# An attention, Fourier mixing and feed-forward kernel on one core: thirteen plain attention tiles instead of eighteen, a fused mask, and weights put together on VectorE

## The chip, the core and the metric

The kernel runs on one core of a Trainium2 chip. A core has a matrix engine (TensorE, PE in the profile), a vector engine (VectorE, DVE), an activation engine (ScalarE, ACT), a general engine (GpSimd, POOL) and a queue engine that issues transfers (SyncE, SP). Each works through its own list of instructions in a fixed order and waits on semaphores for the others. PEld is the loading of the stationary operand into PE. The metric is the device time of one launch in microseconds; the time of the kernel before is the median of three runs.

## What is computed

```python
# q, k, v: (8, 8, 576, 64); w_ch1: (512, 2048); w_ch2: (2048, 512)
scores = (q @ k^T) / 8, kept where 0 <= i - j < 64, else -1e9
attn = softmax(scores)                      # over the last axis
x = (attn @ v), heads side by side          # (8, 576, 512)
u = x + real(fft(fft(x, axis=1), axis=2))
un = (u - mean(u)) / sqrt(var(u) + 1e-6)    # over the last axis
out = u + relu(un @ w_ch1) @ w_ch2
```

The weights arrive as 64-bit numbers (two 32-bit words, low and high); the kernel makes 32-bit floats of them itself.

## The kernel before

**Tiles.** The 8 x 576 rows are 36 tiles of 128 rows, nine to a pair of batches (tile T has place n = T mod 9 in its pair). `attn_tile` does one of them in two halves of 64 queries. It loads k, q and v, brings k and q into the layout that PE wants, multiplies (psc), takes a row's largest score and exponentials (pr), turns the probabilities round (pt), multiplies by v (pa) and normalises (xu). It then takes a radix-4 step for the Fourier part (y) and turns y round (py, yT).

**Plain tiles and tiles in parts.** Tiles below `PRO` (18 here) are plain: float32 all through, with k, q, the probabilities and y turned by TensorE (pk, pq, pp, py). The mask of a plain tile is one more product into the scores' bank (line 542): an identity times the mask, four heads wide. The row maximum is a reduction and a small scaling on VectorE (lines 573 and 574, `top`). Tiles from `PRO` on split each number into two float16 parts, high and low. Their turning is done by transposing DMAs on SP's queue (kst, qbd, pt, py), the splitting by ScalarE, VectorE and GpSimd; their mask is added on VectorE, in the fused step that also takes the row's extreme value (line 564, `masked`). Of these tiles only those whose n stands in `Y_SOON` have y turned by TensorE.

**Fourier part and normalisation.** When a pair's tiles 0 to 4, and then 5 to 8, are done, `fft` transforms one batch (products pg, pz), writes the result to memory (md), and `norm_tile` gathers the rows of it again (mt), adds them to xu, normalises, splits into parts (un, up) and turns them by a DMA into uhl, the input of the feed-forward part.

**Feed-forward part.** `ffn(c)` handles a chunk of 256 rows: 16 steps of a first product (ph, line 1186), relu into parts (hh, lines 1201 and 1204) and a second product (po, line 1167). Chunk 0 is plain (`PLAIN = 1`) and uses the weights in float32; chunks 1 to 17 use weights scaled and split into float16 parts. Chunk c takes tiles 2c and 2c + 1.

**Weights.** Each of the 32 pieces (`weight_piece`) is loaded, its high words shifted and masked by two VectorE instructions (lines 1078 and 1083), its low words scaled by ScalarE (line 1088) and added by GpSimd as 32-bit integers (line 1091). ScalarE then squares the piece for the scale; when all 16 pieces of a matrix are in, `weight_scale` makes the scale and `weight_split` the parts.

**What sets the order.** All of this is handed to a planner (`Plan`), a list of operations with a duration, a priority (a smaller number is sooner), what they read and write, and the rings of buffers they take from. It plays the operations through and writes each engine's instructions in the order that comes out; some operations may go to either of two engines, and `LAZY` and its kin say how much sooner the second must be. `slack` adds to the time at which the planner lets TensorE use what others make. The feed-forward products have the last priority, so they fill TensorE wherever a tile is not ready. Before the first of them stands in the order, warming products (warm, line 1265) are put where the planner sees TensorE idle.

## Time and profile before

| | |
|---|---|
| median of three runs | 1029.38 us (1027.97 to 1029.58) |
| profiled execution, whole | 1027.26 us |
| its span, first to last instruction | 1025.4 us |
| mean granted TensorE clock | 0.994 of full speed |
| first product of feed-forward chunk 0 | at 95.4 us |
| first product of chunk 1 (parts) | at 175.7 us |

The profile is of one execution. Busy time counts an instruction from its start to its modelled end, and TensorE's instructions overlap; so what a group of products costs is read from the distance between its first start and the start of what follows, not from their durations.

### The profile page before, as it was taken

The numbers are of one execution on the slowest core, as the hardware profiler recorded it, in microseconds if no ns is written. First come the engines' busy times: TensorE is split into PE (matmuls) and PEld (weight loads), VectorE is DVE, ScalarE is ACT, GpSimd is POOL, SyncE is SP. The second block draws the span as 40 slices with busy tenths as digits, with TensorE's granted clock in tenths as the row PEclk, the third lists the DMA queues.
The fourth block names the chain that finished last, engine by engine and source line by source line (L and its number), as shares of the span: only waits on it lengthen the run. The fifth ranks groups of instructions, "written<-read, shape, count | busy, mean of one in ns | idle before, by whom it ended". The sixth has DMA issues, their size and how long they took to land.

```text
span 1025.4 us, 22178 instructions
## 1 busy us (share of the span) xinstructions
PE 989.6 (97%) x8743; PEld 709.4 (69%) x8743; DVE 676.6 (66%) x1743; ACT 416.9 (41%) x1060; POOL 188.5 (18%) x200
## 2 busy tenths in 40 slices
PE   8788999999999999989999999999999999999998
PEld 7677767677776767666676676666676667666664
DVE  5799898798756495765775757778686754532121
ACT  5777766545424263233453225343453222211111
POOL 2124432121023020311123203032112100210000
PEclk9999999999999999999999999999999999999999
DMA  8979953337238156486798456686763511220000
GB/s 196 227 187 246 228 164 108 81 74 144 58 96 159 43 100 146 90 166 106 141 134 169 108 104 114 118 174 136 127 114 88 117 20 55 62 53 21 1 22 21
DMA packets 279032, 115.83 MB, mean 113 GB/s; under 512 B 260744, under 2 KB 260872, under 8 KB 278928
## 3 DMA queue, kind: packets, MB, share of 16 engines
q1 hardware_dynamic: 276208, 105.50, 49.9%
q0 software_dynamic: 2720, 8.92, 3.2%
q8 instruction: 69, 1.13, 0.5%
q14 instruction: 35, 0.29, 0.1%
HBM read 54.97 MB, written 14.17 MB: 67 GB/s over the span
## 4 chain that ended last, share of the span: by engine, by line
PE 71%; DVE 12%; DMA 10%; ACT 2%; SPq 2%; issue 2%; POOL 1%; DVEq 0%; ACTq 0%; POOLq 0%
PE ph L1186 31%; PE po L1167 28%; PE pa L646 2%; PE pz L899 2%; PE pg L867 2%; DMA uhl<-up 2%; DMA flex<-in_moe_w_ch 2%; DMA wd<-in_moe_w_ch 2%; PE psc L552 1%; DMA pt<-flex 1%; DVE y L680 1%; DMA va<-in_v 1%; DVE hh L1204 1%; DMA mt<-md,gix 1%; PE psc L545 1%
## 5 line engine op out<-in xcount | busy, mean ns | idle before, releaser
L1186 PE MATMUL ph<-uhl,w0s 128*128 128x256 f16 (+1 forms) x3384 | 426.6, 277 | 9.4 <-DVE hh L1204 9.2
L1167 PE MATMUL po<-w1s,hh 128*128 128x512 f16 (+1 forms) x1696 | 426.8, 389 | 0.0
L1186 PEld LDWEIGHTS <-w0s 128*128 128x128 f16 x3264 | 318.1, 98 | 94.9 <-issue 13.1
L1204 DVE SCALAR_TENSOR_TENSOR hh<-ph,hh 128x256 f16<-128x256 f32 x272 | 114.8, 423 | 235.3 <-ACT hh L1201 223.0
L1201 ACT ACTIVATE hh<-ph 128x256 f16<-128x256 f32 x272 | 104.0, 382 | 401.4 <-PE ph L1186 290.1
L1167 PEld LDWEIGHTS <-hh 128*128 128x128 f16 x1632 | 157.0, 98 | 138.3 <-issue 1.1
L977 POOL DMA_INDIRECT mt<-md,gix x34 | 34.3, 1008 | 111.3 <-DMA md<-mp 90.4
L1001 POOL TENSOR_TENSOR rs<-mv,mhalf 128x1 f32<-128x1 f32 x36 | 21.8, 606 | 178.2 <-DVE mv L997 161.5
L580 ACT ACTIVATE pr<-pr,nm 128x128 f32<-128x128 f32 x144 | 45.6, 390 | 5.7 <-DVE nm L564 5.7
L580 ACT ACTIVATE pr<-psc,nm 128x128 f32<-128x128 f32 x144 | 40.4, 380 | 16.6 <-DVE nm L574 12.5
L545 PEld LDWEIGHTS psc<-kst,qbd 128*128 128x128 f32 x288 | 37.5, 192 | 5.6 <-issue 1.7
L646 PE MATMUL pa<-ve,pt 128*64 128x65 f16 (+1 forms) x720 | 40.9, 209 | 0.1
L646 PE MATMUL pa<-va,pt 128*64 128x65 f16 (+1 forms) x720 | 40.5, 209 | 0.3 <-ACT pt L403 0.2
L545 PE MATMUL psc<-kst,qbd 128*128 128x128 f32 x288 | 38.4, 277 | 1.7 <-ACT qbd L403 1.2
L609 POOL TENSOR_TENSOR flex<-pr,flex 128x512 f16<-128x512 f32 x19 | 23.0, 1215 | 91.5 <-DVE flex L407 54.2
L482 POOL TENSOR_TENSOR flex<-kn,flex 128x512 f16<-128x512 f32 x15 | 17.6, 1176 | 117.8 <-ACT flex L403 92.3
L564 DVE CUSTOM_DVE_ANT_0 pr<-psc,mskb 128x128 f32<-128x128 f32 x144 | 32.8, 285 | 1.4 <-PE psc L552 1.4
L658 DVE TENSOR_TENSOR xu<-pa,rc 128x256 f32<-128x256 f32 x72 | 30.6, 425 | 2.5
L899 PE MATMUL pz<-g,ds__76 97*96 97x257 f16 (+3 forms) x240 | 29.1, 273 | 1.6 <-ACT pr L580 1.1
L680 DVE TENSOR_TENSOR y<-xu 128x256 f32<-128x256 f32 x66 | 29.7, 491 | 1.4 <-PE py L739 0.9
L899 PEld LDWEIGHTS <-ds__76 97*96 97x96 f16 (+1 forms) x240 | 26.8, 124 | 4.2 <-issue 2.6
L403 ACT CAST up<-un 128x512 f16<-128x512 f32 x28 | 17.2, 616 | 28.2 <-DMA uhl<-up 14.3
(155 smaller groups left out, 1214.9 us busy)
## 6 DMA issues: line engine op xcount, KB each, us to landing
wd<-in_moe_w_ch SPq DMA_DIRECT2D x20, 512.0 KB, 4.1
...
```

Source lines behind the costliest of these rows:

```text
L545: nc.tensor.matmul(p_[:, hp], qw, keys(hp, jj), start=False, stop=(hp == 3))
L564: nc.vector.tensor_tensor_reduce(out=t["pr", jj][:, hp], in0=t["ps", jj][:, hp], in1=mskb[:, m : m + P], scale=-0.125, scalar=3.0e38, op0= ...
L580: nc.scalar.activation(pr, src, AF.Exp, bias=t["nm", jj][:, hp : hp + 1], scale=sc_)
L646: nc.tensor.matmul(pa[64 * jj : 64 * jj + 64, hh], pt[:, sl], v_, start=(x == 0), stop=(x == len(mm) - 1))
L658: nc.vector.tensor_tensor(out=xv[:, 4 * hf : 4 * hf + 4], in0=pa[:, :, 0:64], in1=rc.to_broadcast([P, 4, 64]), op=ALU.mult)
L680: eng.tensor_tensor(out=o, in0=p0, in1=p1, op=al)
L899: nc.tensor.matmul(pz[:M, c0:c1], ds_[:NJ, a, c[0] : c[0] + c[1]], t["g", gi][:, b_, c0:c1], start=(x == 0), stop=(x == len(mm) - 1),)
L977: nc.gpsimd.indirect_dma_start(out=mts[T], out_offset=None, in_=mds[pb][0 : HR if n < 4 else 2 * HR], in_offset=bass.IndirectOffsetOnAxis( ...
L1167: nc.tensor.matmul(t["po"][i], l_, r_, start=(f == 0 and x == 0), stop=(f == NKF - 1 and x == len(mm) - 1))
L1186: nc.tensor.matmul(ph, l_, r_, start=(x == 0), stop=(x == len(mm) - 1))
L1201: nc.scalar.activation(t["hh", f][:, 0], ph, AF.Relu)
L1204: nc.vector.scalar_tensor_tensor(out=hh[:, 1], in0=ph, scalar=0.0, in1=hh[:, 0], op0=ALU.max, op1=ALU.subtract)
```

## The change

The change does five things. `PRO` becomes 13: tiles 13 to 17 are done in parts. Since the first tile in parts (13) now is not the first of a pair, two bridges are added: `k_tail` splits the previous tile's keys on VectorE, and `v_next` splits its values there. The mask product of the plain tiles is gone; all tiles use the fused VectorE step. The low words of a weight piece are scaled and added by one VectorE instruction that writes the lower 16 bits of each number; the ScalarE and GpSimd steps are gone. y of tiles with n = 3 is turned by DMA in tiles done in parts. And the numbers that the planner goes by are new.

```diff
-Y_SOON = (3,4,8,)
-LAZY, LAZY_FFT, LAZY_U = 0.2, 0.8, 0.2
-LAZY_E, LAZY_Y = 0.3, 0.4
+Y_SOON = (4, 8)
+LAZY, LAZY_FFT, LAZY_U = 0.4, 0.4, 0.5
+LAZY_E, LAZY_Y = 0.3, 0.8
...
-EARLY, LATER = 80, 0
-PRO = 18
-SLACK = 1.0
+EARLY, LATER = 80, -20
+PRO = 13
+PITCH, FFT_AT, NORM_AT, FFT1 = 8.5, 13, 6, 0
+SLACK = 0.5
...
-W_DMA, W_DMA_STEP, W_CONV, W_SQ, W_SPLIT, W_STEP = -40, 1.25, 40, 80, 60, 0.5
+W_DMA, W_DMA_STEP, W_CONV, W_SQ, W_SPLIT, W_STEP = -40, 1.0, 20, 60, 60, 0.3
...
+        before = (T + 1 if T == PRO else T - 1) % 3
...
+        if T == PRO and n > 0:
+            def k_tail():
+                src = kst32[:, (T - 1) % 3 * 512 : (T - 1) % 3 * 512 + 512].rearrange("p (a s) -> p a s", a=4)
+                dst = kst16[:, before * 1024 : before * 1024 + 1024].rearrange("p (h s) -> p h s", h=H)
+                for h in range(2):
+                    old = src[64 * h : 64 * h + 64, :, 64:128]
+                    hi, lo = (dst[64 * z : 64 * z + 64, h::2, 64:128] for z in range(2))
...
+                    nc.vector.tensor_copy(hi, old)
+                    nc.vector.tensor_tensor(out=lo, in0=old, in1=hi, op=ALU.subtract)
+            op("DVE", 1.6, base + 0.3, k_tail, [BkT[(T - 1) % 3]], [BkT[before], Buf("tail")])
...
         def v_next():
-            nc.sync.dma_start(vbuf[3 - i][64:128], vbuf[i][64:128])
+            if T + 1 == PRO:
+                (hi, lo), v_ = (ve[1 - i][64:128, z] for z in range(2)), va32[i][64:128]
+                nc.vector.tensor_scalar(out=hi, in0=v_, scalar1=VS, scalar2=None, op0=ALU.mult)
+                nc.vector.scalar_tensor_tensor(out=lo, in0=v_, scalar=VS, in1=hi, op0=ALU.mult, op1=ALU.subtract)
+            else:
+                nc.sync.dma_start(vbuf[3 - i][64:128], vbuf[i][64:128])
...
             def score(jj=jj, m=m):
...
-                if whole:
-                    nc.tensor.matmul(p_, idb, mskb[:, None, m : m + P].to_broadcast([P, 4, P]), start=True, stop=False)
                 for hp in range(4 if whole else 0):
                     qw = qbd32[i][:, hp, jj].rearrange("p h s -> p (h s)")
-                    nc.tensor.matmul(p_[:, hp], qw, keys(hp, jj), start=False, stop=(hp == 3))
+                    nc.tensor.matmul(p_[:, hp], qw, keys(hp, jj), start=True, stop=True)
...
-            def top(jj=jj):
-                mx, nm = (sm.tile([P, 4], F32, tag=tag, name=f"{tag}{T}_{jj}") for tag in ("mx", "nm"))
-                t["nm", jj] = nm
-                nc.vector.tensor_reduce(out=mx, in_=t["ps", jj], axis=AX.X, op=ALU.max)
-                nc.vector.tensor_scalar(out=nm, in0=mx, scalar1=-0.125, scalar2=None, op0=ALU.mult)
...
-            if whole:
-                op("DVE", 0.85, base + 2.1 + jj, top, [bs], [bnm], port=False)
-                op("ACT", 1.07, base + 2.5 + jj, expo, [bs, bnm], [bp])
-            else:
-                op("DVE", 0.86, base + 2.1 + jj, masked, [bs, Bmskb], [bp, bnm], port=False)
-                op("ACT", 1.2, base + 2.5 + jj, expo, [bnm], [bp])
+            op("DVE", 0.84, base + 2.1 + jj, masked, [bs, Bmskb], [bp, bnm], port=False)
+            op("ACT", 1.18, base + 2.5 + jj, expo, [bnm], [bp])
...
-            elif i == 2:
-                nc.scalar.mul(lo, lo.bitcast(U32), 2.0**-29)
             else:
-                nc.gpsimd.tensor_tensor(out=dst, in0=dst, in1=lo, op=ALU.add)
+                half_ = wf[x][g].bitcast(U16)[:, 0::2]
+                nc.vector.scalar_tensor_tensor(
+                    out=half_, in0=lo.bitcast(U32), scalar=2.0**-29, in1=half_, op0=ALU.mult, op1=ALU.add
+                )
...
-        op("ACT", 0.58, pr, lambda: conv(2), bw, [br])
-        op("POOL", 1.3, pr - 0.2, lambda: conv(3), [*bw, br], [bf])
+        op("DVE", 0.6, pr - 0.2, lambda: conv(2), bw, [bf])
...
-        base = 8.5 * T + (LATER if T > 4 else -EARLY)
-        plan.slack = SLACK if T >= PRO else 0.0
+        base = PITCH * T + (LATER if T > 4 else -EARLY)
+        plan.slack = SLACK if T >= NT else 0.0
```

How the order changes is shown at three places. First TensorE, at the scores of tile 0 (psc0_0 and psc0_1 are the two halves, mskb the mask, kst the keys). Before:

```order
L542 MATMUL psc0_0_155<-mskb_71,idb_72 128x512
L545 MATMUL psc0_0_155<-kst_80,qbd0_77 128x128 x4
L542 LDWEIGHTS idb_72
L542 MATMUL psc0_1_167<-mskb_71,idb_72 128x512
L545 MATMUL psc0_1_167<-kst_80,qbd0_77 128x128 x4
L462 MATMUL pk1_188<-ident_69,kn1_146 128x128 x4
L595 MATMUL pp0_0_199<-ident_69,pr0_0_154 128x128 x4
```

and after:

```order
L568 MATMUL psc0_0_153<-kst_79,qbd0_76 128x128 x4
L568 MATMUL psc0_1_160<-kst_79,qbd0_76 128x128 x4
L464 MATMUL pk1_172<-ident_69,kn1_134 128x128 x4
L464 MATMUL pq1_186<-ident_69,qn1_144 128x128 x4
L606 MATMUL pp0_0_198<-ident_69,pr0_0_152 128x128 x4
```

The product from the mask and the load of its identity are gone; the four products of the scores stand alone.

Second VectorE, at the weight pieces during the first transform (w0s and w1s hold the weights as they are put together, wd and flex are loaded pieces, mx5_1 and mx6_0 row maxima, pr5_1 the second half of tile 5, pz0 and mp0 belong to the transform). Before:

```order
L1078 TENSOR_SCALAR w1s_86<-flex_79 128x512
L1083 SCALAR_TENSOR_TENSOR w1s_86<-flex_79,w1s_86 128x512
L1078 TENSOR_SCALAR w1s_86<-wd1_3_771 128x512
L573 TENSOR_REDUCE mx6_0_970<-psc6_0_939 128x4
L574 TENSOR_SCALAR nm6_0_971<-mx6_0_970 128x4
L407 COPY qbd1_78<-pq7_931 64x8x64
L1083 SCALAR_TENSOR_TENSOR w1s_86<-wd1_3_771,w1s_86 128x512
L1078 TENSOR_SCALAR w0s_85<-wd0_4_818 128x512
```

and after:

```order
L1101 SCALAR_TENSOR_TENSOR w1s_85<-wd1_3_775,w1s_85 128x512
L1089 TENSOR_SCALAR w0s_84<-wd0_4_886 128x512
L1094 SCALAR_TENSOR_TENSOR w0s_84<-wd0_4_886,w0s_84 128x512
L1101 SCALAR_TENSOR_TENSOR w0s_84<-wd0_4_886,w0s_84 128x512
L1089 TENSOR_SCALAR w0s_84<-wd0_5_949 128x512
L1094 SCALAR_TENSOR_TENSOR w0s_84<-wd0_5_949,w0s_84 128x512
L1101 SCALAR_TENSOR_TENSOR w0s_84<-wd0_5_949,w0s_84 128x512
L1089 TENSOR_SCALAR w0s_84<-wd0_6_1036 128x512
L1094 SCALAR_TENSOR_TENSOR w0s_84<-wd0_6_1036,w0s_84 128x512
L1101 SCALAR_TENSOR_TENSOR w0s_84<-wd0_6_1036,w0s_84 128x512
L587 ISA pr5_1_707,nm5_1_1071<-psc5_1_708,mskb_71 128x128
L587 ISA nm5_1_1071 128x1
```

Each piece now has a third VectorE instruction (line 1101), and four pieces in a row stand ahead of the masked scores of tile 5's second half.

Third SP, from the last piece of transform 3 (mp3_0, written to md1) to the turn of tile 13's normalised rows (up13 into uhl6, the input of feed-forward chunk 6). Before:

```order
L927 DMA md1_3561<-mp3_0_5087 96x512
L929 DMA md1_3561<-mp3_0_5087 1x512
L497 DMA_TRANSPOSE qbd0_77<-flex_79 128x16x64
L427 DMA qn24_5220<-in_q 128x8x64
L1229 DMA out_0<-xu8_1461 128x512
L1229 DMA out_0<-xu9_1637 128x512
L524 DMA ve0_83<-va1_82 64x520
L754 DMA_TRANSPOSE py18_5386<-yp18_5369 128x8x128
L615 DMA_TRANSPOSE pt19_0_5402<-flex_79 128x8x64 x2
L615 DMA_TRANSPOSE pt19_1_5456<-flex_79 128x8x64
L1029 DMA_TRANSPOSE uhl6_4123<-up13_5430 128x8x128
```

and after:

```order
L940 DMA md1_3910<-mp3_0_5677 1x512
L427 DMA qn24_5818<-in_q 128x8x64
L499 DMA_TRANSPOSE qbd1_77<-flex_78 128x16x64
L427 DMA flex_78<-in_v 64x8x64 x2
L765 DMA_TRANSPOSE py19_5868<-yp19_5835 128x8x128
L626 DMA_TRANSPOSE pt20_0_5889<-flex_78 128x8x64
L540 DMA ve1_83<-va1_81 64x520
L499 DMA_TRANSPOSE qbd1_77<-flex_78 128x16x64
L626 DMA_TRANSPOSE pt20_0_5889<-flex_78 128x8x64
L427 DMA kn25_5931<-in_k 128x8x64
L626 DMA_TRANSPOSE pt20_1_5979<-flex_78 128x8x64
L1040 DMA_TRANSPOSE uhl6_4764<-up13_5963 128x8x128
```

The number of transfers between the two is much the same. On TensorE it is another thing: before, transform 3 stands in chunk 4 of the feed-forward part (its last product between steps of f = 12), now it stands in chunk 5 (its last product between steps 8 and 9). Between its last product and the first product of chunk 6 now stand 7 groups of ph (12 products each), 9 of po (6 products each), one tile's output products and two halves of scores.

In all, the changed program has 129 warming products (103 before; 50 of them stand in a row, between transform 0's last product and the turning of tile 5's second half), 36 mask products fewer, and 20 py, 20 pk, 20 pq and 40 pp flips fewer on TensorE. On VectorE 32 instructions of line 1101 are new and ten float32 copies of whole tiles or halves (qbd, kst, pt) are gone.

## Rows read from the trace of the kernel before

**Rows 1.** The page, part 1: busy us (share of the span) x instructions.

```profile
PE 989.6 (97%) x8743; PEld 709.4 (69%) x8743; DVE 676.6 (66%) x1743; ACT 416.9 (41%) x1060; POOL 188.5 (18%) x200
```

**Rows 2.** Windows: stretch, then its length and each engine's busy time, clock, DMA share, GB/s.

```profile
25.00:95.40 70.40, 56.40 (x611) 48.78 (x605) 62.64 (x153) 52.95 (x142) 19.17 (x17) 0.95 0.89 217
95.40:175.70 80.30, 77.35 (x502) 58.22 (x499) 70.98 (x140) 53.84 (x134) 29.13 (x23) 1.00 0.71 176
175.70:1025.40 849.70, 834.01 (x7452) 584.75 (x7450) 529.80 (x1423) 296.85 (x751) 135.07 (x146) 1.00 0.48 96
```

**Rows 3.** Waits of PE, whole program: us in total, times, longest.

```profile
PE ph L1186 <- DVE hh L1204: 9.2, 9, 2.7
```

**Rows 4.** Timeline of PE, 16 to 19 us: start, us, engine, line, operation.

```profile
16.74 0.38 PE L542 MATMUL psc<-mskb,idb 128*128 128x512 bf16 x1
16.96 1.05 PE L545 MATMUL psc<-kst,qbd 128*128 128x128 f32 x8
...
17.85 0.60 PE L462 MATMUL pk<-ident,kn 128*128 128x128 f32 x4
18.31 0.63 PE L739 MATMUL py<-ident,y 128*128 128x128 f32 x4
```

**Rows 5.** Timeline of PE, first and last of tile 3's output products.

```profile
39.41 0.27 PE L646 MATMUL pa<-ve,pt 128*64 128x65 f32 x1
...
40.34 0.22 PE L646 MATMUL pa<-ve,pt 128*64 128x65 f32 x1
```

**Rows 6.** Timeline of PE, tiles 20 to 23, done in parts.

```profile
471.50 0.22 PE L646 MATMUL pa<-ve,pt 128*64 128x65 f16 x1
...
472.28 0.62 PE L552 MATMUL psc<-kst,qbd 128*64 128x128 f16 x16
...
487.25 0.64 PE L552 MATMUL psc<-kst,qbd 128*64 128x128 f16 x16
487.82 1.47 PE L1167 MATMUL po<-w1s,hh 128*128 128x512 f16 x6
```

**Rows 7.** DVE by form, 20 to 265 us: count | busy us, mean ns | idle before.

```profile
L573 DVE TENSOR_REDUCE mx<-psc 128x4 f32<-128x512 f32 x27 | 18.5, 684 | 1.6 <-PE psc L545 1.6
...
L680 DVE TENSOR_TENSOR y<-xu 128x256 f32<-128x256 f32 x24 | 13.1, 587 | 1.0 <-PE py L739 0.9
...
L1083 DVE SCALAR_TENSOR_TENSOR w0s<-wd,w0s 128x512 int32<-128x512 int32 x9 | 6.2, 685 | 0.1
...
L407 DVE COPY qbd<-pq 64x512 f32<-64x512 f32 x7 | 4.8, 689 | 1.5 <-PE pq L462 1.3
```

**Rows 8.** Timeline of DVE, one masked half tile, first row and the next operation.

```profile
492.97 0.28 DVE L564 CUSTOM_DVE_ANT_0 pr<-psc,mskb 128x128 f32<-128x128 f32 x1
...
493.81 0.75 DVE L680 TENSOR_TENSOR y<-xu 128x256 f32<-128x256 f32 x2
```

**Rows 9.** Timelines of DVE and POOL near 83 us.

```profile
82.70 1.84 DVE L680 TENSOR_TENSOR y<-xu 128x256 f32<-128x256 f32 x2
...
82.92 1.35 POOL L1091 TENSOR_TENSOR w0s<-w0s,flex 128x512 int32<-128x512 int32 x1 [2.50 <-DMA mt<-mp]
```

**Rows 10.** Timelines, from a transform's last product to the turn of u; DMA table's row.

```profile
393.52 0.83 PE L899 MATMUL pz<-g,ds__76 97*97 97x257 f16 x6
...
396.79 1.48 PE L1186 MATMUL ph<-uhl,w0s 128*128 128x256 f16 x12
...
399.39 1.47 PE L1186 MATMUL ph<-uhl,w0s 128*128 128x256 f16 x12
...
425.61 1.26 SPq L1029 DMA_TRANSPOSE uhl<-up  x1
...
861.65 0.83 PE L899 MATMUL pz<-g,ds__76 97*97 97x257 f16 x6
...
878.77 22.13 SPq L1029 DMA_TRANSPOSE uhl<-up  x4
...
uhl<-up SPq DMA_TRANSPOSE x34, 3.3
```

More of the change, by code (lines that the diff above doesn't have):

```diff
@@ L17 @@
 U32 = mybir.dt.uint32
+U16 = mybir.dt.uint16
 AF = mybir.ActivationFunctionType
@@ L323, in attn_fft_ffn_kernel @@
     mskb = cp.tile([P, 320], BF16, name="mskb")
-    idb = cp.tile([P, P], BF16, name="idb")
     unit = cp.tile([P, P], F32, name="unit")
@@ L353, in attn_fft_ffn_kernel @@
     wp = [w_[:, 0:16].bitcast(F16).rearrange("p g (z c) -> p g z c", z=2) for w_ in ws]
-    Bid, Bmh, Bmskb, Bgix, Bdd, Bds, Bones, Bidb = (Buf() for _ in range(8))
+    Bid, Bmh, Bmskb, Bgix, Bdd, Bds, Bones = (Buf() for _ in range(7))
     Bq, Bva, Bve = ([Buf() for _ in range(2)] for _ in range(3))
@@ L380, in to_parts @@
         for i in range(2):
-            fresh = i == PRO % 2
+            fresh = PRO % NT == 0 and i == PRO % 2
             def ones(i=i, fresh=fresh):
@@ L387, in ones @@
                     nc.gpsimd.memset(ve[i][64:128], 0.0)
-            op("POOL", 0.7, 100, ones, writes=[Bva[i], Bve[i]] if fresh else [Bva[i]])
+            op("POOL", 0.7, PITCH * PRO - 25, ones, writes=[Bva[i], Bve[i]] if fresh else [Bva[i]])
     def pieces(src, b0, g0, n):
@@ L450, in keys @@
             w = kw // 64
-            own, old = T % 3 * w + 2 * h, (T - 1) % 3 * w + 2 * h + 1
+            own, old = T % 3 * w + 2 * h, before * w + 2 * h + 1
             step = old - own
@@ L505, in attn_tile @@
                 op("DMA", TURN, base + 0.7, lambda j=j: q_turn(j), Bfl[4:6], [Bq[i]], lat=2.8)
+        if T == PRO and n > 0:
[5 more added lines that the diff above has]
+                    hi, lo = (dst[64 * z : 64 * z + 64, h::2, 64:128] for z in range(2))
+                    if h:
+                        odd = sb([P, 4, 64], F32, "tail", f"odd{T}")[0:64]
+                        nc.vector.tensor_copy(odd, old)
+                        old = odd
+                    nc.vector.tensor_copy(hi, old)
+                    nc.vector.tensor_tensor(out=lo, in0=old, in1=hi, op=ALU.subtract)
+            op("DVE", 1.6, base + 0.3, k_tail, [BkT[(T - 1) % 3]], [BkT[before], Buf("tail")])
         def v_part(z):
@@ L523, in v_next @@
         def v_next():
-            nc.sync.dma_start(vbuf[3 - i][64:128], vbuf[i][64:128])
+            if T + 1 == PRO:
[4 more added lines that the diff above has]
+                nc.sync.dma_start(vbuf[3 - i][64:128], vbuf[i][64:128])
         op("DMA", 0.55, base - 4 if whole else base + 3.2, v_own, [Bva[i]], [Bve[i]], lat=2.8)
-        if n + 1 < NT:
+        if n + 1 < NT and T + 1 == PRO:
+            op("DVE", 1.1, base + 6, v_next, [Bva[i]], [Bve[1 - i]])
+        elif n + 1 < NT:
             op("DMA", 0.55, base - 3.9 if whole else base + 6, v_next, [Bva[i]], [Bve[1 - i]], lat=2.8)
@@ L555, in score @@
                             )
-            rd = [Bq[i], bkT, *([] if jj or n == 0 else [BkT[(T - 1) % 3]])]
-            op("PE", 1.15 if whole else 0.6, base + 2 + jj, score, [*rd, Bidb, Bmskb] if whole else rd, [bs, bp])
+            rd = [Bq[i], bkT, *([] if jj or n == 0 else [BkT[before]])]
+            op("PE", 0.95 if whole else 0.52, base + 2 + jj, score, rd, [bs, bp])
             def masked(jj=jj, m=m):
@@ L578, in expo @@
                     pr = t["pr", jj][:, hp]
-                    src, sc_ = (t["ps", jj][:, hp], 0.125) if whole else (pr, -1.0)
-                    nc.scalar.activation(pr, src, AF.Exp, bias=t["nm", jj][:, hp : hp + 1], scale=sc_)
-            if whole:
-                op("DVE", 0.85, base + 2.1 + jj, top, [bs], [bnm], port=False)
-                op("ACT", 1.07, base + 2.5 + jj, expo, [bs, bnm], [bp])
-            else:
-                op("DVE", 0.86, base + 2.1 + jj, masked, [bs, Bmskb], [bp, bnm], port=False)
-                op("ACT", 1.2, base + 2.5 + jj, expo, [bnm], [bp])
+                    nc.scalar.activation(pr, pr, AF.Exp, bias=t["nm", jj][:, hp : hp + 1], scale=-1.0)
+            op("DVE", 0.84, base + 2.1 + jj, masked, [bs, Bmskb], [bp, bnm], port=False)
+            op("ACT", 1.18, base + 2.5 + jj, expo, [bnm], [bp])
             if whole:
@@ L1074, in conv @@
                 wf[x].append(sb([P, 512], F32, "big", f"wf{x}_{g}"))
-            dst = wf[x][g].bitcast(I32) if i != 2 else None
+            dst = wf[x][g].bitcast(I32)
             if i == 0:
@@ L1241, in attn_fft_ffn_kernel @@
         if n in (4, 8):
-            base += 13
+            base += FFT_AT + (FFT1 if T == 8 else 0)
             fft(2 * pb + n // 8, base)
             for i, m in enumerate(range(0, 4) if n == 4 else range(4, 9)):
-                norm_tile(NT * pb + m, base + 6 + i + (EARLY if T == 4 and i > 1 else 0))
+                norm_tile(NT * pb + m, base + NORM_AT + i + (EARLY if T == 4 and i > 1 else 0))
         if T == 4:
```

5 lines of the change are left out of this document (2 added, 3 removed).

## Prediction

> **What bounds the kernel now.** I read the page's busy line first: TensorE is busy 989.6 of 1025.4 us, VectorE 676.6 [rows 1]. A pipelined TensorE that reads 97% may still hide stalls, so next come the windows, cut where feed-forward chunk 0 and chunk 1 begin (95.4 and 175.7 us). They show two regimes [rows 2]. From 175.7 us to the end TensorE is busy 834.0 of 849.7 us at full clock, and VectorE 529.8: the feed-forward products fill every gap that a tile leaves, and TensorE's own work is the time. Ahead of that it is not so. From 25 to 95.4 us TensorE is busy 56.4 of 70.4 us (and that with warming products counted), VectorE 62.6; from 95.4 to 175.7 us VectorE is busy 71.0 of 80.3. There the tiles and the weights' conversion on VectorE set the pace. The waits of TensorE confirm it: the longest entry is 9.2 us in nine waits for VectorE's part of relu (hh) [rows 3], 1% of the span.
>
> So a microsecond less on TensorE is worth a microsecond behind 175.7 us and about nothing ahead of it; a microsecond more on VectorE is worth up to one ahead of 175.7 us and nothing behind.
>
> **TensorE's part.** Prices are distances from start to start. A mask product costs 16.96 - 16.74 = 0.22 us, the f32 scores of a half 17.85 - 16.96 = 0.89, a flip of four 18.31 - 17.85 = 0.46 [rows 4]. The output products of a plain tile are sixteen pairs from 39.41 to 40.34 plus the last pair, 0.99 [rows 5]. In parts, a tile's output products take 472.28 - 471.50 = 0.78 and a half's scores 487.82 - 487.25 = 0.57 [rows 6].
>
> A plain tile without mask and y is thus 2 x 0.89 + 4 x 0.46 (k, q, two of probabilities) + 0.99 = 4.61 us, one in parts 2 x 0.57 + 0.78 = 1.92: 2.69 less, times five tiles 13.4. The 36 mask products give 7.9, the five flips of y that go (20 products) 2.3. Together 23.6 us. Of it, 23 mask products (5.1) and two flips of tile 13 (0.9) stood ahead of chunk 1, where they are worth nothing; and the new order puts a half's scores of tile 11 and a flip and half the output of tile 10 (0.9 + 0.5 + 0.5 = 1.9) behind chunk 1's start instead of ahead of it. Behind it remain 23.6 - 6.0 - 1.9 = 15.7 us, which I count in full. The 26 added warming products stand ahead, in gaps, and cost nothing: what they cover is idle time. If that cover goes (a product in the way of a tile that is ready) they cost at most 26 times the 0.11 us that half a mask product (256 columns of 512) takes, 2.9 us.
>
> **VectorE's part, ahead of chunk 1.** Before the first relu of chunk 1 stand 31 of the 32 new additions of low words. The trace does not show this operation. The nearest row is the two-input step on the same 512 numbers, 0.685 us [rows 7], which I take: 31 x 0.685 = 21.2 us. As ends I allow half of that (10.6 us, an estimate) and, for a step that GpSimd disturbs as in [rows 9], 1.1 us more.
>
> The mask on VectorE is nearly free: a masked half takes 493.81 - 492.97 = 0.84 us [rows 8], the reduction that it replaces 0.68 [rows 7] plus a small scaling. About six copies of 0.69 [rows 7] leave VectorE ahead of chunk 1: -4.1.
>
> What GpSimd no longer does matters too. The pair of y steps that takes 1.84 us at 82.70 ran while GpSimd added low words for 1.35 us at 82.92 [rows 9]; undisturbed the pair takes 0.75 [rows 8]. So one collision costs VectorE about 1.1 us. With 32 additions gone the relief lies between 0 and 35 us; VectorE is not always at a two-input step when GpSimd adds, and 24 such y steps have a mean of 587 ns [rows 7], some 0.2 above half of the quiet pair, which is 5 us in one group alone. With the other groups I take 14, some 13 collisions.
>
> [...]
>
> Net: +21.2 - 4.1 - 14 = +3 us for VectorE ahead of chunk 1, with ends at -18 (all relief) and +17 (none). ScalarE loses 32 scalings; it waits for others in this stretch and gains nothing for the end. Weight loads are one after the other in nearly the old order on SP; chunk 1 still needs all sixteen pieces of the first matrix. I take +3.
>
> **A wait that the order adds, at chunk 6.** Chunk 6 needs tile 13, and tile 13 needs transform 3. In the new order TensorE has, between that transform's last product and chunk 6's first, 7 groups of ph and 9 of po, scores of two halves and one tile's outputs. A ph and a po together take 399.39 - 396.79 = 2.60 us [rows 10], so 8 x 2.60 + 2 x 0.57 + 0.78 = 22.7 us. What has to happen in it is seen twice in the trace: from 861.65 to the turn's issue at 878.77 is 17.1 us, with an idle SP queue; for this very transform, from 393.52 to 425.61, 32.1 us [rows 10], but with nobody in a hurry and tile work put first. Add 3.3 us for landing [rows 10]: 20.4 or 35.4. Cover less chain is +2.3 or -12.7. Behind a waiting first product of chunk 6 stands all of TensorE, since the fill-in work of chunk 5 is used up. The new queue still has eleven transfers, six of them transposes, ahead of the turn. Near the quiet row I take a chain of about 25 us, a wait of 2 us.
>
> **The sum.** It is made against the profiled execution's 1027.3 us: 1027.3 - 15.7 + 3 + 2 = 1016.6. That execution lies within the three timed runs, 2.1 under their median of 1029.38; I leave the forecast at 1016, 1.3% under the median. Other waits behind chunk 1 (15.7 us of idle TensorE there now) I take as unchanged.
>
> **Rivals.**
>
> *The front shrinks too.* If GpSimd's absence gives VectorE back much of 35 us, the front is no longer VectorE's, and TensorE's whole 23.6 us count: 1027.3 - 23.6 = about 1004. For it: the collision at 83 us, and 88% busy time on VectorE in front of chunk 1. Against: VectorE also waits there for loads and for TensorE, and the 50 warming products in a row that now stand ahead of tile 5's second half say that TensorE still has nothing to do for a while.
>
> *The tile work falls behind the feed-forward part.* The chain of transform 3 stays near its 35.4 us. Then TensorE waits 12.7 at chunk 6 in place of 2: 1016.6 + 10.7 = 1027, no change to speak of. For it: tiles 13 to 17 go through transposing DMAs on one queue, and transform 3 comes a chunk later on TensorE. Against: nothing made the old chain hurry.
>
> *Slower: the conversion on VectorE holds up chunk 1.* Place: the weights' pieces, all of which the scale waits for. Price: 21.2 us of additions without relief, and the four pieces in a row ahead of tile 5's second half delay the tiles too, so that nothing of it is hidden: 1027.3 - 15.7 + 21.2 + 2 = 1035. It decides from the point at which chunk 1 starts 13.7 us later than 175.7, that is after 189.4 us. Against it: rows 9, and ten fewer copies.
>
> **Chances.** The forecast 0.58 (its own range 1009 to 1023), the front that shrinks 0.20, the tile work behind 0.12, the conversion that holds 0.10. The range takes in the first rival's centre and most of the second's: 1003 to 1028. Runs of this kernel agree to within 0.2%, so that is where I put "no change" (1027.3 to 1031.4). Faster: 0.58 + 0.20 and a quarter of the second rival, 0.81. Same: most of the second rival and a little of the third, 0.10. Slower: 0.09.
>
> **What would show it.** Chunk 1's first product at 174 to 182 us says that the front stayed; near 170 the first rival, past 189 the third. TensorE's time from there to the end should be 834 to 838 us, some 13 to 16 less than 849.7. The new line 1101 should take near 0.69 us, and the y steps ahead of 175 us should lose their long ones. A wait of ph for the turn of uhl at chunk 6's start, of up to 4 us, fits; 10 us or more is the second rival. If VectorE's relu becomes TensorE's releaser for much over 10 us in all, the planner's smaller slack has let TensorE run ahead of what feeds it, and I have missed it.

## The result and the profile after

The changed kernel takes 1013.93 us (median of four, 1012.65 to 1017.26) where the kernel before takes 1028.98: ratio 0.986, 95% interval 0.9835 to 0.9885. The forecast was 1016, with 1003 to 1028 as its range. The profiled execution of the changed kernel is one of 1014.19 us; times below are its own unless another run is named.

The page's busy line [rows 1] reads, after the change:

```profile
PE 975.3 (96%) x8793; PEld 692.1 (68%) x8793; DVE 671.6 (66%) x1972; ACT 417.3 (41%) x1044; POOL 205.8 (20%) x211
```

TensorE is busy 14.3 us less, and the span is 13.0 us shorter: 1.3 us of TensorE time turned idle. The windows, cut at the same events as [rows 2] (first product of chunk 0, of chunk 1, end):

```profile
25.00:93.10 68.10, 55.64 (x555) 47.57 (x553) 60.33 (x193) 42.24 (x111) 5.38 (x6) 0.87 0.86 222
93.10:170.10 77.00, 77.00 (x518) 58.43 (x517) 69.34 (x204) 48.87 (x129) 8.14 (x8) 1.00 0.72 190
170.10:1012.40 842.30, 822.34 (x7536) 569.25 (x7535) 528.91 (x1510) 310.76 (x768) 188.96 (x184) 1.00 0.55 106
```

Chunk 1 starts at 170.1 us, 5.6 earlier; from there to the end it is 842.3 us, 7.4 less than 849.7. So the total came out right (13.0 of span saved, 10.7 forecast) from two parts that were both off: the front was to grow by 3, the back to shrink by 15.7 less a wait of 2. GpSimd's busy time between 25 us and chunk 1 falls from 48.3 us (19.17 + 29.13) to 13.5. Between the two chunks TensorE now has no idle time at all: 77.00 of 77.00 us, against 77.35 of 80.30 before.

The waits of TensorE, whole program; the first row answers to [rows 3]:

```profile
PE ph L1197 <- DVE hh L1215: 8.6, 13, 1.7
PE pa L657 <- DMA pt<-flex: 5.1, 4, 3.2
PE pp L606 <- ACT pr L595: 3.7, 1, 3.7
...
PE ph L1197 <- DMA uhl<-up: 0.3, 1, 0.3
```

Relu holds TensorE no longer than before, and the wait for the turn of u, forecast at 2 us, is 0.3. New is the second row: output products that wait for turned probabilities (pt). The longest of these, in TensorE's timeline at tile 15:

```profile
304.78 0.64 PE L575 MATMUL psc<-kst,qbd 128*64 128x128 f16 x16 [0.23 <-DMA qbd<-flex]
...
308.73 0.22 PE L657 MATMUL pa<-va,pt 128*64 128x65 f16 x1 [3.20 <-DMA pt<-flex]
...
309.76 2.74 PE L1197 MATMUL ph<-uhl,w0s 128*128 128x256 f16 x12
312.29 0.94 PE L1178 MATMUL po<-w1s,hh 128*128 128x512 f16 x3
```

Twelve ph products take 1.47 us elsewhere in this trace; behind the 3.2 us wait they take 2.74, so one stall was paid twice: the granted clock from 309.1 to 312.3 us is 0.51, where it was 1.00 up to 309.1. SP's queue shows why pt is late:

```profile
298.41 2.58 SPq L626 DMA_TRANSPOSE pt<-flex  x2
301.05 1.31 SPq L499 DMA_TRANSPOSE qbd<-flex  x1
302.47 1.10 SPq L938 DMA_DIRECT2D md<-mp  x1
303.61 0.29 SPq L940 DMA_DIRECT2D md<-mp  x1
303.94 1.19 SPq L626 DMA_TRANSPOSE pt<-flex  x1
```

The last turn of the probabilities of tile 15 is issued at 303.94, behind a turn of q and two writes of transform 2, and TensorE gets it 4.8 us later. Before, tile 15 was plain and used no such turn.

VectorE by form, 20 to 265 us, as [rows 7] (count | busy us, mean ns):

```profile
L691 DVE TENSOR_TENSOR y<-xu 128x256 f32<-128x256 f32 x22 | 8.8, 443 | 0.2
...
L1101 DVE SCALAR_TENSOR_TENSOR w0s<-wd,w0s 128x512 uint16<-128x512 uint32 x10 | 7.4, 739 | 0.3
...
L1094 DVE SCALAR_TENSOR_TENSOR w0s<-wd,w0s 128x512 int32<-128x512 int32 x10 | 6.9, 691 | 0.3
```

The new addition lasts 739 ns; neighbours overlap, and from start to start the 31 of them ahead of chunk 1 take 19.7 us, 0.64 each. The y step falls from 587 to 443 ns in the mean: the long ones of [rows 9] are gone.

### The profile page after: what moved, and what is told of

The parts are those of the page before. It is cut to its first block, busy times and chain, and to the rows that moved or that the text cites. A ratio compares the mean times of both kernels' runs of the same rounds, so it can differ in the third digit from the quotient of the medians.

```text
span 1012.4 us, 22555 instructions
## 1 busy us (share of the span) xinstructions
PE 975.3 (96%) x8793; PEld 692.1 (68%) x8793; DVE 671.6 (66%) x1972; ACT 417.3 (41%) x1044; POOL 205.8 (20%) x211
## 4 chain that ended last, share of the span: by engine, by line
PE 73%; DMA 10%; DVE 9%; SPq 3%; ACT 2%; issue 2%; POOL 1%; DVEq 0%; ACTq 0%; POOLq 0%
PE ph L1197 31%; PE po L1178 28%; PE pa L657 3%; PE pg L878 2%; PE pz L910 2%; PE psc L568 2%; DMA uhl<-up 2%; DMA pt<-flex 2%; PE psc L575 2%; DMA kn<-in_k 1%; DMA mt<-md,gix 1%; DVE hh L1215 1%; SPq L626 1%; DMA qn<-in_q 1%; DVE y L691 1%
## 5 line engine op out<-in xcount | busy, mean ns | idle before, releaser
L1197 PEld LDWEIGHTS <-w0s 128*128 128x128 f16 x3264 | 318.5, 98 | 96.8 <-issue 14.3
L595 ACT ACTIVATE pr<-pr,nm 128x128 f32<-128x128 f32 x288 | 91.3, 393 | 16.3 <-DVE nm L587 16.3
L587 DVE CUSTOM_DVE_ANT_0 pr<-psc,mskb 128x128 f32<-128x128 f32 x288 | 65.7, 286 | 15.9 <-PE psc L568 11.8
L1035 POOL TENSOR_TENSOR up<-un,up 128x512 f16<-128x512 f32 x33 | 39.0, 1183 | 70.4 <-ACT up L403 63.6
L620 POOL TENSOR_TENSOR flex<-pr,flex 128x512 f16<-128x512 f32 x25 | 30.0, 1202 | 109.5 <-ACT flex L403 90.7
L484 POOL TENSOR_TENSOR flex<-kn,flex 128x512 f16<-128x512 f32 x19 | 22.7, 1197 | 83.6 <-ACT flex L403 82.1
L403 ACT CAST flex<-pr 128x512 f16<-128x512 f32 x38 | 23.5, 620 | 27.7 <-DMA pt<-flex 25.5
L568 PE MATMUL psc<-kst,qbd 128*128 128x128 f32 x208 | 29.8, 293 | 2.5 <-ACT qbd L403 1.2
L657 PEld LDWEIGHTS <-pt 128*64 128x64 f16 x1104 | 20.8, 112 | 14.0 <-issue 7.2
L568 PEld LDWEIGHTS psc<-kst,qbd 128*128 128x128 f32 x208 | 26.9, 203 | 4.5 <-issue 1.9
```

The costliest lines, as they stand in the source:

```text
L568: nc.tensor.matmul(p_[:, hp], qw, keys(hp, jj), start=True, stop=True)
L587: nc.vector.tensor_tensor_reduce(out=t["pr", jj][:, hp], in0=t["ps", jj][:, hp], in1=mskb[:, m : m + P], scale=-0.125, scalar=3.0e38, op0= ...
L595: nc.scalar.activation(pr, pr, AF.Exp, bias=t["nm", jj][:, hp : hp + 1], scale=-1.0)
L657: nc.tensor.matmul(pa[64 * jj : 64 * jj + 64, hh], pt[:, sl], v_, start=(x == 0), stop=(x == len(mm) - 1))
L1035: eng.tensor_tensor(out=t["up"][:, 1], in0=t["un"], in1=t["up"][:, 0], op=ALU.subtract)
L1197: nc.tensor.matmul(ph, l_, r_, start=(x == 0), stop=(x == len(mm) - 1))
```

## The experiments

Each of the twelve was timed beside the kernel before, in three groups, each on a chip of its own: rows 1 to 4 of the table, rows 5 to 8, rows 9 to 12. The kernel before has medians of 1026.3, 1027.9 and 1026.4 us in them, and its 35 times in the third group spread from 1020.2 to 1032.3; so runs of different groups are best compared by the ratio. The last three columns are of one profiled execution each. The first row is the base, with which the others are compared.

| run | ratio to before, 95% | median us | chunk 1 at | PE busy | span less PE busy |
|---|---|---|---|---|---|
| changed kernel again | 0.9858 (0.9833-0.9884) | 1011.6 | 170.2 | 970.4 | 38.6 |
| low words old way | 0.9820 (0.9799-0.9841) | 1008.8 | 171.8 | 974.6 | 33.9 |
| GpSimd addition added | 0.9953 (0.9937-0.9969) | 1022.6 | 178.0 | 974.9 | 46.6 |
| 18 plain tiles | 0.9978 (0.9953-1.0002) | 1023.8 | 168.7 | 983.2 | 35.6 |
| mask on TensorE | 0.9872 (0.9831-0.9912) | 1014.4 | 170.2 | 975.9 | 33.7 |
| all numbers old | 1.0116 (1.0072-1.0160) | 1039.4 | 174.6 | 980.8 | 57.4 |
| before + new numbers | 0.9971 (0.9947-0.9996) | 1025.9 | 177.7 | 989.6 | 35.5 |
| pt told to land later | 1.0060 (1.0031-1.0090) | 1032.2 | 167.3 | 973.6 | 59.4 |
| mask and low words old | 1.0036 (1.0014-1.0058) | 1031.3 | 170.1 | 980.5 | 50.8 |
| 18 plain, low words old | 0.9958 (0.9930-0.9985) | 1023.7 | 172.9 | 985.7 | 37.2 |
| 18 plain, mask on TensorE | 0.9971 (0.9950-0.9993) | 1025.6 | 170.0 | 992.4 | 33.0 |
| margins old | 0.9988 (0.9967-1.0010) | 1025.0 | 174.6 | 975.0 | 45.9 |

For the profiled kernel before the last three columns are 175.7, 989.6 and 35.8.

**The base.** No edit.

> The changed kernel once more, unaltered, as the base of the three others. Both theories: 1014 us within 2, chunk 1's first product at 170 us, 842 us from there to the end, and again a wait of about 5 us in all of pa for the turned probabilities, the longest of them at tile 15.

1011.6 us beside a kernel before of 1026.3, a little below what was expected. Chunk 1 starts at 170.2 us. The waits for pt are 2.4 us here, not 5, and the longest, at the same tile, is 1.1; from chunk 1 to the end it is 838.8 us. So the wait varies between executions, and the back's saving is 7 to 11 us.

**Low words the old way.**

```
-  VectorE: half_ = lo * 2^-29 + half_   (16-bit numbers)
+  ScalarE: lo = lo * 2^-29 ;  GpSimd: dst = dst + lo   (32-bit)
```

> The changed kernel, but with the low words made the old way: ScalarE scales them, GpSimd adds them as 32-bit numbers. Theory by VectorE's account: the front loses 18.9 us of additions on VectorE and gets 15.6 us of collisions back, so chunk 1 starts between 167 and 171 us, 842 us follow, and the total is 1011 to 1015. Rival (the relief from collisions is what shrank the front, the additions fit into VectorE's gaps): chunk 1 starts at 176 to 185 us and the total is 1020 to 1029. The y steps of two inputs get long ones again in both.

2.8 us faster than the base (1006.96 to 1010.26 against 1010.78 to 1013.32). Chunk 1 starts at 171.8 us, 1.6 later, so the rival falls; the theory's bands (167 to 171, total 1011 to 1015) are missed too, by little. From chunk 1 on it is 836.7 us, and the waits for pt are gone. The y steps are long again:

```profile
L691 DVE TENSOR_TENSOR y<-xu 128x256 f32<-128x256 f32 x18 | 12.3, 723 | 0.1
```

So 19.7 us of additions bought about as much relief. This version beats both kernels; that it does so behind chunk 1, where only one of the 32 low-word steps stands, speaks for the order that the planner found and against the conversion as the reason, which no run tests by itself.

**A useless GpSimd addition beside each low-word step.**

```
+  GpSimd: lo = lo + lo
```

> The changed kernel with one useless GpSimd addition more behind each of the 32 low-word steps (the raw piece added to itself where nothing reads it again), all else in the same order. It measures the collisions by themselves. Theory: VectorE's excess over its median durations ahead of chunk 1 goes from 1.3 us back to 10 to 17, and since VectorE sets the pace there chunk 1 starts 8 to 15 us later, at 178 to 185 us; total 1022 to 1029. Rival (VectorE has 18.5 us of idle time ahead of chunk 1 that takes the collisions in): excess as above, but chunk 1 at 170 to 173 us, total 1014 to 1017.

As the theory has it: chunk 1 comes 7.8 us later, the total is 11.1 more. The excess (the time by which VectorE's instructions ahead of chunk 1 outlast the median of their kind) is 12 to 17 us, by how kinds are told apart, and 1 in the base. VectorE by form, 20 to 178 us:

```profile
L691 DVE TENSOR_TENSOR y<-xu 128x256 f32<-128x256 f32 x18 | 10.7, 634 | 0.2
L1094 DVE SCALAR_TENSOR_TENSOR w0s<-wd,w0s 128x512 int32<-128x512 int32 x10 | 9.8, 978 | 0.3
...
L1094 DVE SCALAR_TENSOR_TENSOR w1s<-flex,w1s 128x512 int32<-128x512 int32 x6 | 6.3, 1051 | 0.2
```

Two of the four groups of a step that takes 691 ns in the changed kernel take 978 and 1051 here (the other two 695 and 772), and nothing else was added to them. So the collisions are real. Ahead of chunk 1 VectorE's busy time grows by 14.9 us over the base (142.8 to 157.7) and its idle time shrinks by 7.1 (27.4 to 20.3): half of the collisions reach chunk 1, and the rival's idle time takes in the other half. Of the 7.8 us 2.2 fall ahead of chunk 0 and 5.6 between the chunks, where TensorE has 4.1 us of idle time in this run and none in the base.

**18 plain tiles again.**

```
-PRO = 13
+PRO = 18
```

> The changed kernel with 18 plain tiles again instead of 13; mask, low words and numbers stay as changed. Theory (the step to parts is worth little here, since the tiles in parts wait for transposes and run at a lower granted clock after these waits): behind chunk 1 5 to 8 us more, 847 to 850; ahead of chunk 1 up to 4 us more for some copies on VectorE; total 1018 to 1026, and no wait of pa for turned probabilities at 300 to 400 us. Rival (the prices from start to start hold): 13.4 + 2.3 - 0.9 = 14.8 us more behind chunk 1, total 1029 to 1033.

12.2 us slower than the base. 1023.8 us itself lies in the theory's band; but the forecasts stood against 1014 us, 4 to 12 and 15 to 19 more, and counted so the run lies between the two, nearer the first's upper end. TensorE is busy 12.8 us more; chunk 1 starts 1.5 us earlier, and from there on it is 850.1 us, the theory's upper end.

**Mask on TensorE for the 13 plain tiles.**

```
+  TensorE: p_ = idb x mask (start), then the scores on top
-  VectorE: fused mask, minimum and scaling
+  VectorE: reduction and scaling
```

> The changed kernel (1011.6 us beside the kernel before at 1026.3 in the runs of this day), but the mask of the 13 plain tiles is again a product on TensorE, with the plain reduction on VectorE: 26 products of 0.22 us are added, 23 of them ahead of chunk 1, and VectorE loses some 26 x 0.1 us. Theory (between chunk 0 and chunk 1 TensorE has become the bound, busy 77.0 of 77.0 us): the masks between the chunks count, chunk 1 starts 2.5 to 5 us later, at 172.7 to 175.2 us, and the total is 3 to 6 us more, 1014.5 to 1017.5. Rival (as predicted, VectorE sets the pace ahead of chunk 1): chunk 1 at 168 to 171 us and only the three masks behind it count, total 1010 to 1012.5.

Chunk 1 comes at 170.2 us, as the rival has it, which is the prediction's own reading, with 22 mask products more ahead of it. The total, 1014.4 us, lies between the two forecasts, in a group in which the kernel before is 1.5 us slower; by the ratio it can't be told from the base. Windows of this run:

```profile
25.00:93.00 68.00, 55.80 (x576) 46.85 (x575) 61.64 (x148) 43.76 (x116) 4.45 (x6) 0.97 0.91 226
93.00:170.20 77.20, 76.72 (x511) 57.95 (x510) 70.98 (x153) 46.00 (x120) 8.15 (x8) 1.00 0.65 179
```

Sixteen of the masks stand ahead of chunk 0, where the base's TensorE has some 20 us of idle time and 17 of warming products: there they cost nothing (chunk 0 starts at 92.6 us here, at 92.9 in the base). The other six stand between the chunks (6 x 0.22 = 1.3 us), and the stretch grew by 0.2. But this order also puts a half's scores and six products of a transform (1.8 us) behind chunk 1's start and four flips (0.5 us) ahead of it, so that TensorE's work between the chunks is about the same. Whether the masks would count there, where TensorE is never idle, this run does not decide.

**All of the planner's numbers old.**

```
-Y_SOON = (4, 8);      LAZY, LAZY_FFT, LAZY_U = 0.4, 0.4, 0.5
-LAZY_E, LAZY_Y = 0.3, 0.8;  EARLY, LATER = 80, -20;  SLACK = 0.5 (from T >= NT)
+Y_SOON = (3, 4, 8);   LAZY, LAZY_FFT, LAZY_U = 0.2, 0.8, 0.2
+LAZY_E, LAZY_Y = 0.3, 0.4;  EARLY, LATER = 80, 0;    SLACK = 1.0 (from T >= PRO)
 and the six W_... of the weights
```

> The changed kernel with the planner's numbers of before (dates, slack, priorities), and 13 plain tiles. Theory (the numbers only decide where waits fall; the 12 us less of TensorE work behind chunk 1 stays): total 1008 to 1018, behind chunk 1 TensorE busy 820 to 823 us, and a wait at chunk 6 or for turned probabilities of at most 5 us. Rival (the new numbers are what lets the tiles in parts keep up with the feed-forward part): waits of TensorE for transposes of over 10 us behind chunk 1, total 1020 or more.

The edit also has TensorE turn y again in the tiles in parts with n = 3. 27.8 us slower than the base, slower even than the kernel before: the rival's total. Its mark, waits for transposes of over 10 us, is missed (6.8), and so are the theory's (TensorE is busy 830.0 us behind chunk 1, not 820 to 823). TensorE's idle time behind chunk 1 is 33.7 us, 17.0 in the base. The longest waits:

```profile
PE ph L1197 <- DVE hh L1215: 15.3, 16, 3.2
PE pp L606 <- ACT pr L595: 9.5, 2, 6.6
PE ph L1197 <- DMA uhl<-up: 6.8, 2, 4.4
```

**The new numbers alone, on the kernel before.** The same edit backwards, on the kernel before.

> The kernel before with the planner's new numbers alone (18 plain tiles, mask on TensorE, low words by GpSimd). Theory (numbers carry little of the gain): the ratio to the kernel before is 0.997 to 1.005, chunk 1 starts between 173 and 179 us. Rival (the 5.6 us that the front lost come from the numbers, which load and convert weights closer together): chunk 1 at 169 to 172 us, ratio 0.994 to 0.996.

As the theory has it: 0.3% faster, chunk 1 at 177.7 us. Numbers that are worth 27.8 us with the change are worth 2 without it.

**The planner told that pt lands later.**

```
-  op("DMA", HTURN, base + 4.2 + jj, p_turn, ..., lat=1.8)
+  op("DMA", HTURN, base + 4.2 + jj, p_turn, ..., lat=4.0)
```

> The changed kernel with the planner told that turned probabilities land 4.0 us after their issue instead of 1.8. Theory (the waits of pa for them, 2.4 to 5.3 us, and the 1.0 us that ph then loses at the lower granted clock near 305 us come from an order made with too short a landing time): these waits fall below 1 us, TensorE's idle time behind chunk 1 falls by 2 to 5 us, total 1007 to 1010. Rival (the queue is full there, so another wait takes the place): idle time behind chunk 1 within 1.5 us of the changed kernel's 12.9, total 1010.5 to 1014.

The wait for pt is gone and another takes its place, at a price that neither theory had: 20.6 us slower. Its longest entry, and the row of the longer of the two waits in TensorE's timeline:

```profile
PE ph L1198 <- DMA uhl<-up: 22.9, 2, 12.8
```

```profile
411.57 0.83 PE L911 MATMUL pz<-g,ds__75 97*97 97x257 f16 x6
443.26 6.68 PE L1198 MATMUL ph<-uhl,w0s 128*128 128x256 f16 x36 [12.82 <-DMA uhl<-up]
```

This is chunk 6 waiting for transform 3, the prediction's second rival. That the wait is nearly its 12.7 us is luck: the chain from the transform's last product to chunk 6 is 30.9 us long (412.4 to 443.3) under a cover of 18.0, where the rival had 35.4 and 22.7. The timelines of this kernel and then of the changed one show where the chain grew, from the normalised rows of tile 13 (un) to their parts (up):

```profile
429.69 0.55 DVE L1017 TENSOR_SCALAR un<-xu,mv,rs 128x512 f32<-128x512 f32 x1 [0.34 <-POOL rs L1013]
432.21 1.28 SPq L766 DMA_TRANSPOSE py<-yp  x1
436.31 0.62 ACT L404 CAST up<-un 128x512 f16<-128x512 f32 x1 [6.87 <-DVE va L531]
436.93 1.27 POOL L989 DMA_INDIRECT mt<-md,gix  x1 [0.19 <-issue]
438.23 1.17 POOL L1036 TENSOR_TENSOR up<-un,up 128x512 f16<-128x512 f32 x1
```

```profile
429.35 0.55 DVE L1016 TENSOR_SCALAR un<-xu,mv,rs 128x512 f32<-128x512 f32 x1 [0.34 <-POOL rs L1012]
430.82 0.61 ACT L403 CAST up<-un 128x512 f16<-128x512 f32 x1
431.92 1.16 POOL L1035 TENSOR_TENSOR up<-un,up 128x512 f16<-128x512 f32 x1
```

The rows are ready at the same time within 0.4 us, but ScalarE makes their high part 5.5 us later (436.31 against 430.82), and GpSimd the low part, on which the turn waits, 6.3 us later (438.23 against 431.92). The parts of u (up) and of y (yp) take turns in a ring of one buffer. In this order a y comes first: its turn (py) is issued at 432.21, and not before it has landed may ScalarE write, which it does at 436.31, 4.1 us behind the issue. The label names a step of VectorE (va), which is no operand of this one; the semaphore that ScalarE waits for, and GpSimd with it, is that of y's turn. In the changed kernel the last turn of y was issued at 422.9. Behind ScalarE a gather takes GpSimd's place for 1.3 us more. That is half of the wait; the other half is the cover, 6.6 us shorter than the changed kernel's 24.6, and why the order left less work there was not followed up. After the wait the 36 ph products take 6.68 us instead of some 4.1 (24 take 2.78 at full clock); the granted clock from 400 to 500 us is 0.90 in the mean, and 1.00 in the 100 us on either side. Chunk 1 starts at 167.3 us here, 2.9 earlier than in the base, though nothing ahead of it was changed but the order.

**Mask and low words both old, 13 plain tiles.** Both edits above together.

> 13 plain tiles and the new numbers, but mask products on TensorE and low words by ScalarE and GpSimd, both as before. Alone each moved chunk 1's start by at most 1.6 us (170.2 with both new, 171.8 with old low words, 170.2 with old masks). Theory (the two stand in for each other: VectorE's collisions and TensorE's masks fall into one chain, and the front grows only with both): chunk 1 at 175 to 179 us, total 1015 to 1020. Rival (they add up, and the rest of the front's loss comes from elsewhere): chunk 1 at 171 to 173 us, total 1008 to 1013.

Chunk 1 at 170.1 us: the theory falls, and the rival's band (171 to 173) is missed by little. But the total is 1031.3 us, above both forecasts, because of waits behind chunk 1:

```profile
PE ph L1212 <- DVE hh L1230: 19.7, 15, 3.8
```

The longest of them, in the timelines of VectorE and of TensorE:

```profile
425.34 0.42 DVE L1230 SCALAR_TENSOR_TENSOR hh<-ph,hh 128x256 f16<-128x256 f32 x1
430.93 0.68 DVE L1015 TENSOR_TENSOR xu<-xu,mt 64x511 f32<-64x511 f32 x1 [5.16 <-DMA mt<-md,gix]
...
433.43 0.41 DVE L1230 SCALAR_TENSOR_TENSOR hh<-ph,hh 128x256 f16<-128x256 f32 x1
...
434.74 0.41 DVE L1230 SCALAR_TENSOR_TENSOR hh<-ph,hh 128x256 f16<-128x256 f32 x1
```

```profile
435.20 2.72 PE L1212 MATMUL ph<-uhl,w0s 128*128 128x256 f16 x12 [3.81 <-DVE hh L1230]
```

VectorE stands 5.16 us at a step that wants gathered rows (mt), and two relus (hh) stand behind it and the steps that follow from it; TensorE goes on when the second ends. TensorE's wait names relu; its cause is the gather.

**18 plain tiles with old low words, and with old masks.** The edits above with PRO = 18.

> 18 plain tiles, new numbers, mask on VectorE, low words by ScalarE and GpSimd as before. With both new chunk 1 starts at 168.7 us and the total is 1023.8, with both old (numbers alone) 177.7 and 1025.9. Theory (low words cost what they cost with 13 plain tiles, 1.6 us in front): chunk 1 at 169.5 to 171.5 us, total 1019 to 1024. Rival (with 18 plain tiles, and more copies on VectorE, the collisions with GpSimd are what makes those 9 us): chunk 1 at 174 to 179 us, total 1025 to 1030.

> 18 plain tiles, new numbers, mask products on TensorE as before, low words on VectorE. 36 mask products, some 12 of them behind chunk 1, are 2.6 us there. Theory (ahead of chunk 1 the masks are hidden, as with 13 plain tiles): chunk 1 at 168 to 170 us, total 1025 to 1028. Rival (the masks on TensorE make the 9 us between both new and both old): chunk 1 at 173 to 178 us, total 1029 to 1035.

1023.7 and 1025.6 us: totals as the theories have them, neither rival. Chunk 1 moves to 172.9 (the theory's band ended at 171.5) and 170.0. With 18 plain tiles all four combinations of mask and low words lie at 0.996 to 0.998. Chunk 1 does move there: 177.7 us with both old, 168.7 with both new, so that with 18 plain tiles either one brings most of what both bring, as the theory of the run with both old had it for 13.

**The margins alone old.**

```
-LAZY, LAZY_FFT, LAZY_U = 0.4, 0.4, 0.5 ;  LAZY_Y = 0.8
+LAZY, LAZY_FFT, LAZY_U = 0.2, 0.8, 0.2 ;  LAZY_Y = 0.4
```

> The changed kernel with one group of the planner's numbers as before: the margins by which a step that may run on either engine goes to VectorE or to GpSimd (all four that the change altered). It moves some 34 instructions from GpSimd to VectorE. With all numbers as before the time was 1039.4 us, VectorE had 36 us more, TensorE waited 15.3 us for relu. Theory (this work on VectorE holds up relu, and that is most of the 27 us): waits for relu 12 us or more, VectorE busy over 695 us, total 1020 to 1035. Rival (the dates and the slack are what matters, VectorE has room behind chunk 1): waits for relu under 10 us, total 1009 to 1016.

13.4 us slower, about half of what all numbers together cost. The time is the theory's, but both marks of its mechanism are missed: VectorE is busy 691.5 us, not over 695, and the waits for relu are 9.8 us, not 12 or more. Chunk 1 comes 4.4 us later, and behind it TensorE has 7.3 us more idle time, spread:

```profile
PE ph L1197 <- DVE hh L1215: 9.8, 13, 2.4
PE pa L657 <- DMA pt<-flex: 4.3, 8, 1.0
```

## Why the prediction was right, step by step

**The signs.** Of the prediction's signs two failed: chunk 1 came at 170.1 us, not at 174 to 182 (near 170 was the first rival's mark), and from there to the end it was 842.3 and 838.8 us, not 834 to 838. The others held: the new addition at 739 ns, y steps without long ones, no wait of over 4 us at chunk 6, relu at 8.6 us.

**The two regimes: right, but the line between them moved.** Behind chunk 1 TensorE's work is the time. Ahead of it GpSimd collisions given back to VectorE moved chunk 1 by 7.8 us, and the 16 masks ahead of chunk 0 cost nothing. Between the chunks, where the prediction had VectorE alone set the pace, TensorE's idle time went from 2.9 us to none, so that TensorE is full there too.

**TensorE's 15.7 us behind chunk 1: right in kind, too large.** Measured 7.4 and 10.9 us. From start to start, in the profiled runs of before and after, what goes is near its price or above it: f32 scores, flips and output products of the tiles 20.9 us, masks 2.6, y flips 2.6. What comes is dearer: the parts' scores 5.6 and outputs 6.4 instead of 9.6 together, and ph and po take 3.0 more, in part at the lower clock behind waits. The step that failed is the price of a tile in parts, 1.92 us: its 0.78 for the output products is an unbroken tile's, and the 23 tiles in parts of the changed kernel take 0.94 each (0.85 in the kernel before). In the changed kernel many are done in two halves, as this one:

```profile
440.16 0.22 PE L657 MATMUL pa<-ve,pt 128*64 128x65 f16 x1
...
440.67 1.48 PE L1197 MATMUL ph<-uhl,w0s 128*128 128x256 f16 x12
...
442.08 0.22 PE L657 MATMUL pa<-ve,pt 128*64 128x65 f16 x1
...
442.58 1.49 PE L1197 MATMUL ph<-uhl,w0s 128*128 128x256 f16 x12
```

0.51 + 0.50 = 1.01 us, against [rows 6]; others stop for pt in the middle. The second failure is that other waits behind chunk 1 were taken as unchanged: TensorE's idle time there went from 15.7 to 20.0 us, 5.1 of it the new wait for pt (in the base run 17.1). By the direct test, undoing the five tiles costs 12.2 us, with an interval of some 4 us to either side by the ratios.

**VectorE's +3 ahead of chunk 1: wrong in sign.** Its own terms were near: additions 19.7 us (21.2 forecast), copies about -6 (-4.1), relief some 16 (14 forecast; the excess ahead of chunk 1 is 14 to 18 us before and 1 or less after). They give about -2 where I had +3. Measured, VectorE's busy time ahead of chunk 1 falls by 4.1 us (146.8 to 142.7), because work that the sum left out went too: two masked halves stand behind chunk 1's start, as the prediction counted for TensorE alone, and VectorE does four of the weights' splits there in place of six (1.7 us for the two halves, 1.7 for the two splits). The other 1.5 us are idle time of VectorE. On TensorE's side 2.9 of the 5.6 us are waits for others between the chunks, the longest of them this one of the kernel before, for a sum on VectorE that the weights' scale needs (few):

```profile
PE py L739 <- DVE few L1117: 2.5, 1, 2.5
```

Which part of the change this comes from stays open. With the new numbers alone chunk 1 starts at 177.7 us, 2 later than before; with the mask on VectorE as well at 172.9, or with the low words there at 170.0; with both at 168.7; with the five tiles in parts too at 170.2. So with 18 plain tiles mask and low words take 9 us off the front. With 13 plain tiles undoing either or both moves chunk 1 by 1.6 at most, and the margins by 4.4; and a later date for pt alone moves it by 2.9. These are single executions, and the order that the planner makes of a change moves chunk 1 about as much as the change does. That the numbers pay because GpSimd is free of its additions was not tried; the run with the old low words gives GpSimd its additions back under the new numbers and loses 1.6 us in front, which speaks against it.

Two readings of the prediction were off besides, with little weight: the profiled execution of 1027.3 us lies 0.7 under the lowest of the three timed runs and not among them, and a y step by itself lasts 420 ns in the changed kernel, not half of an overlapping pair, so that the relief in that group is 4 us and not 5.

The run with the added GpSimd addition puts the cost of 32 additions at some 15 us of VectorE time (142.8 to 157.7 us busy ahead of chunk 1), well below the 36.6 us by which GpSimd's busy time grows (206.4 to 243.0). By what the two engines hold each other up, the runs do not show. The new low-word addition takes 739 ns for 512 numbers, no less than the 32-bit step's 691; of the half price that the prediction allowed as an end nothing is seen.

**Chunk 6: the chain right, the wait of 2 us not there.** The chain of transform 3 in the changed kernel, [rows 10], in the timelines of TensorE and SP:

```profile
412.00 0.82 PE L910 MATMUL pz<-g,ds__75 97*97 97x257 f16 x6
...
437.45 2.78 PE L1197 MATMUL ph<-uhl,w0s 128*128 128x256 f16 x24
```

```profile
433.29 1.30 SPq L1040 DMA_TRANSPOSE uhl<-up  x1
```

20.5 us to the issue, 3.3 to land by [rows 10]: 23.8 us, where I took 25, under a cover of 24.6, where I took 22.7. The slack of 0.8 us is an estimate, since the landing is the median of the kernel before; in the run with the later pt it took 3.8. So little slack is why it is fragile: there the buffer shared with y and the gather cost 6.3 us and the cover is 6.6 shorter; with the mask on TensorE chunk 6 waits 1.9 us, with all numbers old 4.4.

**The rivals.** The front that shrinks came in part: chunk 1 is at its mark, and between the chunks the front is no longer VectorE's alone. Its price is far off, 1004 us against 1014, since the relief was some 16 us and not 35. The tile work that falls behind did not come, and is the mechanism nearest at hand: it came in the run with the later pt, by way of the shared buffer and a shorter cover. The conversion that holds chunk 1 did not come, and is far: with the collisions added to the additions chunk 1 came at 178.0 us, not past 189.4.

So the total was right by luck: two errors, 8.6 us in front and 6.3 behind (842.3 against the 836.0 that 849.7 - 15.7 + 2 gives), offset each other. The direction of the part behind chunk 1 (7 to 11 us of the 15.7) was not luck.

**Where the gain comes from.** The five tiles in parts: 11 to 15 us in three of the four combinations at the new numbers (both new 1023.8 to 1011.6, low words old 1023.7 to 1008.8, mask old 1025.6 to 1014.4; by the ratios 10 to 14). In the fourth, both old, they cost 5 (1025.9 to 1031.3; by the ratios 7), and with the old numbers the changed kernel is slower than before. So neither the tiles nor the numbers give the gain by themselves. TensorE's work shrinks in these too, by 9 us; waits take it back. Why the planner's order comes out that much worse there, beyond the waits shown, stays open.
